# Second mixture: first pair by plain blocks, products ahead of sums, gates behind, operand steps in another order

## The chip, the cores and the metric

One core of one Trainium2 chip runs the kernel. Its engines are TensorE (PE in the rows, its weight loads PEld), VectorE (DVE), ScalarE (ACT), GpSimd (POOL) and SyncE (SP), which issues the transfers. Each engine works through its own queue in program order and waits there for what another engine has still to do. The metric is device microseconds of one execution; times are medians of several.

## The reference

Three stages follow each other. The change touches only the third.

```python
x = attention(q, k, v)                       # 4 x 576 tokens, 8 heads of 64 -> x: 2304 x 512
x = moe(x, phi, w1, w2)                      # first mixture: 8 experts of 4 slots each
# x is now  c @ slot_out : 2304 x 32 times 32 x 512
# second mixture:
logits = x @ w_gate                          # 2304 x 8
P = np.exp(logits - logits.max())
for _ in range(8):                           # the gates
    P /= P.sum(1, keepdims=True) + 1e-09
    P /= P.sum(0, keepdims=True) + 1e-09
    P *= N / E
out = 0
for e in range(8):
    h = np.maximum(x @ w1[e], 0.0)           # 2304 x 1024
    out += P[:, e:e + 1] * (h @ w2[e])       # 2304 x 512
```

All of it is in 4-byte floats.

## The kernel before

The second mixture (from line 777 on) never forms x. It takes x as c times the 32 slot outputs: `a_part` and `a_sum` (lines 802 to 823) form slot_out times w1[e] for one half of its 1024 columns each (`ap`, `as`), and `z_mm` (868) multiplies that by c to get the hidden layer of a pair. A **pair** is 256 tokens, two tiles of 128. An expert has nine pairs, eight experts have 72. A pair has 8 `z` matmuls, four for each half (z1 and z0, one buffer in PSUM for each).

The product with w2[e] is done by Strassen's scheme in Winograd's form: the pair's hidden layer is cut in 2 x 2 blocks a11, a12, a21, a22 and w2[e] in 2 x 2 blocks, and seven block products j0 to j6 (`product`, 918) stand in for eight. Every operand is split in a high and a low part (each rounded to the fast float form), so that a product is 12 matmuls: 84 for a pair. For the splitting, ACT makes the high part (`z_hi`, `s_hi`, and `w_hi` for the weights), DVE or POOL the low part (`z_lo` on DVE, `s_lo` on POOL, `w_lo` on either). Four operands are sums of blocks s1 to s4 (`z_sum` on DVE; h22 and h11 are copies of blocks on ACT, `z_f`, which two of the sums read). Of the weights, t1 to t4 are sums of blocks (`w_sum`); W0 to W6 are the operands of j0 to j6.

The results are added to `acc` on DVE by five updates for a pair: `up_a` behind j1, `up_b` behind j3, `up_d` behind j4, `up_c` behind j5, `up_e` behind j6 (940 to 954). j3 and j5 write to the bank that `up_a` and `up_b` read, j6 to the one that `up_d` reads. Four banks of PSUM (`qy`) serve the products, `ap`, `as` and the gates.

The order is written out by hand: every step of the mixture is entered into `plan` with a time in units of one product (12 matmuls), seven units for a pair, and the steps are issued in the order of these times (lines 1053 to 1118). With t0 the time of a pair's j0, line 1065 puts its z1 matmuls into t0-4 to t0-3, line 1066 its z0 matmuls into t0-3 to t0-2, and a table behind them has the operand steps. In the first expert the gates (`gate`, 976; `sink`, 1002) run as 130 side steps, one every five or six products, from the first pair on (`side_step`, 1070); their additions and divisions are on DVE. The weights of the next expert are loaded (`load_w1`, `load_w2`), multiplied (`a_part`, `a_sum`) and split (`w_plan`, 1089 to 1115) between the products of the expert before.

The first pair of all has nothing to run beside it: `a_part` and `a_sum` for both halves, t1 to t4, all the splits of its weights and its seven products follow each other directly behind the first mixture (1024 to 1043 and 1098 to 1102).

Of the kernel before, what the change touches and what calls it, by code (L numbers as in the profile page):

```python
# [46 lines left out]
WIDE_Q = frozenset((0, 2, 3, 9, 12, 13,))  # L47


@with_exitstack  # L50
def attn_moe_moe_kernel(
# [13 lines left out]
    nc = tc.nc  # L65
# [726 lines left out]
    def load_w1(e, i):  # L792
        t = wp.tile([128, KD, 512], FP32, name="w1s", tag="w")
        nc.sync.dma_start(out=t, in_=w1b[e, :, 512 * i:512 * i + 512].rearrange("(j p) f -> p j f", p=128))
        w1t[e, i] = t

    def load_w2(e, i):
        t = wp.tile([128, HF, DM], FP32, name="w2s", tag="w")
        nc.sync.dma_start(out=t, in_=w2b[e, 512 * i:512 * i + 512, :].rearrange("(j p) d -> p j d", p=128))
        w2t[e, i] = t  # L800

    def a_part(e, a):

        ap = qy.tile([128, 512], FP32, name="ap", tag="y")
        for j in range(KD):
            nc.tensor.matmul(
                out=ap[32 * j:32 * j + 32, :], lhsT=soT[:, j, 0, :], rhs=w1t[e, a][:, j, :], start=True, stop=True
            )
        s = op_.tile([128, 2, 512], FP32R, name="aps", tag="o")
        nc.scalar.activation(out=s[:, 0, :], in_=ap, func=ACTF.Copy)  # L810
        nc.vector.tensor_tensor(out=s[:, 1, :], in0=ap, in1=s[:, 0, :].bitcast(FP32), op=ALU.subtract)  # L811
        apt[e, a] = s

    def a_sum(e, a):
        ap = qy.tile([128, 512], FP32, name="as", tag="y")
        s = apt.pop((e, a))
# [7 lines left out]

    apt = {}
# [323 lines left out]
```

## Time and profile before

| what | value |
|---|---|
| median of 3 executions | 1137.19 us (1134.47 to 1137.31) |
| the profiled execution | 1138.38 us |
| its span, first to last instruction | 1136.5 us |
| mean granted TensorE clock | 0.961 |
| second mixture | from about 223 us to the end |
| PE, DVE, ACT, POOL busy over the span | 91%, 67%, 50%, 56% |

The page gives busy times of the whole span first, then 40 slices of it, the queues of the transfers, the chain of work that ended last, and the costliest groups of instructions. Busy shares over the span mix stages with different limits. The views by stretches of time (one row for each stretch) and the timelines of single engines show each stage by itself. In a timeline, the bracket at a row's end is the idle time of the engine before that row and what ended it.

### The profile page before, as it was taken

The numbers are of one execution on the slowest core, as the hardware profiler recorded it, in microseconds if no ns is written. First come the engines' busy times: TensorE is split into PE (matmuls) and PEld (weight loads), VectorE is DVE, ScalarE is ACT, GpSimd is POOL, SyncE is SP. The second block draws the span as 40 slices with busy tenths as digits, with TensorE's granted clock in tenths as the row PEclk, the third lists the DMA queues.
The fourth block names the chain that finished last, engine by engine and source line by source line (L and its number), as shares of the span: only waits on it lengthen the run. The fifth ranks groups of instructions, "written<-read, shape, count | busy, mean of one in ns | idle before, by whom it ended". The sixth has DMA issues, their size and how long they took to land.

```text
span 1136.5 us, 22853 instructions
## 1 busy us (share of the span) xinstructions
PE 1035.0 (91%) x9231; PEld 943.4 (83%) x9231; DVE 758.6 (67%) x1322; ACT 564.7 (50%) x1084; POOL 639.0 (56%) x488
## 2 busy tenths in 40 slices
PE   6888888859888999999989998999899989998998
PEld 5766653348778989998989998899889988998998
DVE  4997943176889766566667666666766676666665
ACT  5886731043335555654555455445544554455443
POOL 5654521065265637753965486558646763777353
PEclk9898978859999999999999999999899999999999
DMA  9999998930001300130013002201120120000111
GB/s 193 170 184 224 243 361 297 386 125 33 1 1 38 112 1 2 38 112 1 1 48 102 1 4 73 75 1 38 41 73 1 38 83 30 1 1 20 38 57 57
DMA packets 95901, 93.83 MB, mean 83 GB/s; under 512 B 59060, under 2 KB 64820, under 8 KB 95796
## 3 DMA queue, kind: packets, MB, share of 16 engines
q1 hardware_dynamic: 95796, 92.37, 29.5%
q8 instruction: 73, 1.20, 0.5%
q14 instruction: 32, 0.26, 0.1%
HBM read 87.64 MB, written 4.72 MB: 81 GB/s over the span
## 4 chain that ended last, share of the span: by engine, by line
PE 52%; DVE 20%; ACT 8%; issue 7%; DMA 7%; POOL 4%; SPq 2%; ACTq 0%; DVEq 0%; POOLq 0%
PE y L925 41%; DVE ft L898 6%; PE z L873 4%; DVE ot L888 4%; DVE acc L936 4%; DMA kn<-in_k_dram 3%; ACT wt L857 2%; ACT ft L894 2%; POOL wt L861 2%; PE h L711 1%; ACT ot L904 1%; DMA w2s<-in_moe_w_dram 1%; DVE bd L405 1%; DMA wa<-in_moe_w_dram 1%; POOL ot L908 1%
## 5 line engine op out<-in xcount | busy, mean ns | idle before, releaser
L925 PE MATMUL y<-wt,ot 128*128 128x256 f32 x6048 | 822.6, 286 | 50.6 <-DVE acc L936 36.3
L925 PEld LDWEIGHTS y<-wt,ot 128*128 128x128 f32 x6048 | 779.0, 193 | 74.8 <-issue 45.3
L908 POOL TENSOR_TENSOR ot<-ft,ot 128x512 fp32r<-128x512 f32 x288 | 372.9, 1315 | 343.9 <-ACT ot L904 337.6
L936 DVE SCALAR_TENSOR_TENSOR acc<-y,pg,acc 128x256 f32<-128x256 f32 x315 | 201.7, 640 | 150.1 <-PE y L925 149.9
L904 ACT ACTIVATE ot<-ft 128x512 fp32r<-128x512 f32 x288 | 166.8, 624 | 182.5 <-DVE ft L898 167.2
L898 DVE SCALAR_TENSOR_TENSOR ft<-z,ft 128x512 f32<-128x512 f32 x288 | 196.8, 683 | 12.2 <-ACT ot L884 11.7
L888 DVE SCALAR_TENSOR_TENSOR ot<-z,ot 128x512 fp32r<-128x512 f32 x216 | 148.0, 685 | 48.0 <-ACT ft L894 47.2
L884 ACT ACTIVATE ot<-z 128x512 fp32r<-128x512 f32 x216 | 128.1, 593 | 91.0 <-PE z L873 84.3
L873 PE MATMUL z<-c,a4s 128*128 128x256 f32 x576 | 163.1, 286 | 1.4 <-DVE a4s L823 1.4
L894 ACT ACTIVATE ft<-z 128x512 f32<-128x512 f32 x144 | 86.0, 597 | 148.8 <-DVE ot L888 79.2
L873 PEld LDWEIGHTS z<-c,a4s 128*128 128x128 f32 x576 | 110.8, 194 | 1.9 <-DVE a4s L823 1.9
L861 POOL TENSOR_TENSOR wt<-w2s,wt 128x1024 fp32r<-128x1024 f32 x23 | 56.8, 2482 | 10.8 <-ACT wt L857 10.8
L861 DVE TENSOR_TENSOR wt<-ts,wt 128x1024 fp32r<-128x1024 f32 x17 | 33.6, 1983 | 23.6 <-ACT wt L857 23.6
L861 POOL TENSOR_TENSOR wt<-ts,wt 128x1024 fp32r<-128x1024 f32 x15 | 42.3, 2839 | 5.9 <-ACT wt L857 5.9
L391 POOL TENSOR_TENSOR pl<-pl,l 128x384 f32<-128x384 f32 x16 | 13.3, 831 | 53.0 <-DVE l L387 51.5
L405 DVE STREAM_TRANSPOSE bd<-pl 32x384 f32<-32x384 f32 x64 | 36.4, 569 | 1.4
L847 POOL TENSOR_TENSOR ts<-w2s 128x1024 f32<-128x1024 f32 x15 | 37.0, 2464 | 0.0
L857 ACT ACTIVATE wt<-ts 128x1024 fp32r<-128x1024 f32 x32 | 32.8, 1046 | 6.0 <-DVE ts L847 6.0
L936 DVE SCALAR_TENSOR_TENSOR acc<-y,acc 128x512 f32<-128x512 f32 (+1 forms) x45 | 26.0, 577 | 11.7 <-PE y L925 11.5
L811 DVE TENSOR_TENSOR aps<-ap,aps 128x512 fp32r<-128x512 f32 x16 | 11.1, 692 | 28.3 <-ACT aps L810 28.3
L242 PE MATMUL kps<-ident,kn 96*128 96x96 f32 x96 | 13.2, 282 | 16.2 <-DMA kn<-in_k_dram 16.0
L257 ACT ACTIVATE kt<-kps 64x576 f32<-64x576 f32 x32 | 20.5, 642 | 13.9 <-DVE kd L249 13.7
(178 smaller groups left out, 826.8 us busy)
## 6 DMA issues: line engine op xcount, KB each, us to landing
wa<-in_moe_w_dram SPq DMA_DIRECT2D x32, 1024.0 KB, 9.8
w1s<-in_moe_w_dram SPq DMA_DIRECT2D x16, 1024.0 KB
w2s<-in_moe_w_dram SPq DMA_DIRECT2D x16, 1024.0 KB, 5.8
vw<-in_v_dram SPq DMA_DIRECT2D x62, 96.0 KB, 6.2
kn<-in_k_dram SPq DMA_DIRECT2D x32, 144.0 KB, 6.3
vg<-in_v_dram SPq DMA_DIRECT2D x16, 288.0 KB
out_dram<-acc SPq DMA_DIRECT2D x18, 256.0 KB, 2.0
qn<-in_q_dram SPq DMA_DIRECT2D x20, 144.0 KB, 6.6
```

Of the source, the lines that this page charges most:

```text
L405: nc.vector.transpose(out=bds[u % 2][32 * c:32 * c + 32, :, c, :], in_=U[u]["pl"][32 * c:32 * c + 32])
L857: nc.scalar.activation(out=t[:, 0], in_=w_of(e, i), func=ACTF.Copy)
L861: eng.tensor_tensor(out=t[:, 1], in0=w_of(e, i), in1=t[:, 0].bitcast(FP32), op=ALU.subtract)
L873: nc.tensor.matmul(out=zt[n, k][:, f, :], lhsT=a4s[:, e % 2, f0:f0 + 128], rhs=c4[:, BLK * b:BLK * b + BLK], start=True, stop=True,)
L884: nc.scalar.activation(out=t[:, 0], in_=zv(n, i, k), func=ACTF.Relu)
L888: nc.vector.scalar_tensor_tensor(out=t[:, 1], in0=zv(n, i, k), scalar=0.0, in1=t[:, 0].bitcast(FP32), op0=ALU.max, op1=ALU.subtract)
L894: nc.scalar.activation(out=t, in_=zv(n, i, k), func=ACTF.Relu)
L898: nc.vector.scalar_tensor_tensor(out=t, in0=zv(n, i, k), scalar=0.0, in1=ft[n, other], op0=ALU.max, op1=op)
L904: nc.scalar.activation(out=t[:, 0], in_=ft[n, name], func=ACTF.Copy)
L908: nc.gpsimd.tensor_tensor(out=t[:, 1], in0=ft[n, name], in1=t[:, 0].bitcast(FP32), op=ALU.subtract)
L925: nc.tensor.matmul(out=yt[n, bank][:, HD * half:HD * half + HD], lhsT=ot[n, name][:, l, f, :], rhs=tt[e, j][:, r, f, :], start=(m == 0 and ...
L936: nc.vector.scalar_tensor_tensor(out=o, in0=in_, scalar=pg[:, t, e:e + 1] if e else 1.0, in1=o, op0=ALU.mult, op1=ALU.add)
```

## The change

- The first pair is done by the plain scheme: eight products of blocks, 96 matmuls, with a fourth a-block (a21) and an eighth weight block (W7) in place of the four sums s1 to s4. It takes eight units where the other pairs take seven, so that all later times are one unit further on.
- `a_part` runs for both halves, the second half first, and `a_sum` follows for both. The gates' product `gp` and its split, which stood between them, become steps of the plan at 2.21 and 4.46, inside the first pair. `stack_r` and `ones` are made on POOL.
- The gates' side steps begin with the second pair, every five products, and are 118 in place of 130 (three tiles of the logits in one step). The logits, their transposed maxima and the maximum for all partitions share one bank.
- Within every pair all operand steps, the z1 matmuls and the updates have new times (`P`). z1 is issued 0.89 units earlier.
- The weights' steps have new times (`W0` for the first expert, `W` for the others). W1's low part goes from POOL to DVE. `a_part` begins about 0.9 units earlier in the expert than before, `a_sum` is 2.75 units later.
- The dictionaries of tiles become `Ring` objects, and `need` and `made` are assertions on the order; neither adds an instruction.

```diff
+P = {'z1': 4.89, 'z0': 3,
+ 'a12h': -2.46, 'a12l': -1.64, 'h22': -2.22, 'a11h': -2.12, 's1': -1.61, 'h11': -1.79, 'a11l': -1.49,
+ 'a22h': -1.24, 's2': -1.27, 'a22l': -0.3, 's2h': -0.05, 's2l': 0.24, 's4': 0.15, 's1h': -0.41, 's3': 0.65,
+ 's1l': 0.79, 's3h': 0.8, 's3l': 1.04, 's4h': 2.2, 's4l': 2.56,
+ 'ua': 2.01, 'ub': 4.22, 'ud': 5.2, 'uc': 6.19, 'ue': 7.47}
+P0 = ((-3.45, -3.16, -2.01, 1.77, -1.6, 2.91, -0.95, 0.59, 5.1, 6.1, 8.71, 8.08), ...
+W0 = {'0h': -9.21, '6h': -6.84, '1h': -4.85, '7h': -0.9, '2h': 2.44, '3h': 2.25, '4h': 3.75, '5h': 4.98,
+ 'gp': 2.21, 'g': 4.46,
+ '0l': (-8.05, 0), '6l': (-5.5, 1), '1l': (-2.28, 0), '7l': (1.08, 1),
+ 't1': (-7.68, 0), 't2': (-0.28, 1), 't4': (0.56, 1), 't3': (3.48, 0),
+ '2l': (2.5, 1), '3l': (5.33, 0), '4l': (4.74, 0), '5l': (5.44, 1)}
+W = {'ap': 14.61, 'as': 19.65,
+ 't1': (22.65, 1), 't2': (33.72, 1), 't4': (38.68, 1), 't3': (40.91, 1),
+ '0h': 44.89, '1h': 41.33, '2h': 57.7, '3h': 59.91, '4h': 56.58, '5h': 61.69, '6h': 66.19,
+ '0l': (48.68, 1), '1l': (45.62, 0), '2l': (59.61, 1), '3l': (62.44, 1), '4l': (59.48, 0), '5l': (65.8, 0),
+ '6l': (67.58, 1), 'ld1': 9.4, 'ld2': 9.71}
...
+    def plain(n, i, c, k, m):
+        if m == 0 and k == PLAIN_K[0]:
+            yt.tile((n, i, c), [128, DM], FP32, "y", "y")
+        f, p = divmod(m, 3)
+        l, r = ((0, 0), (1, 0), (0, 1))[p]
+        nc.tensor.matmul(
+            out=yt[n, i, c][:, 0:HD], lhsT=ot[n, f"a{i + 1}{k + 1}"][:, l, f, :],
+            rhs=tt[n // NB, PLAIN_T[k][c]][:, r, f, :],
+            start=(m == 0 and k == PLAIN_K[0]), stop=(m == 3 * HF - 1 and k == PLAIN_K[1]),
+        )
...
-    a_part(0, 0)
-    gp = qy.tile([128, E], FP32, name="gp", tag="y")
...
-    a_sum(0, 0)
-    a_part(0, 1)
...
-    a_sum(0, 1)
+    for i in (1, 0):
+        a_part(0, i)
+    for i in (1, 0):
+        a_sum(0, i)
...
-        t0 = 7 * n
+        t0 = 7 * n + min(n, nplain)
         for f in range(HF):
-            at(t0 - 4 + (f + 0.5) / 4, z_mm, n, 1, f)
-            at(t0 - 3 + (f + 0.5) / 4, z_mm, n, 0, f)
+            at(t0 - P["z1"] + (f + 0.5) / 4, z_mm, n, 1, f)
+            at(t0 - P["z0"] + (f + 0.5) / 4, z_mm, n, 0, f)
...
-                if e == 0 and (84 * n + 12 * j + m) % 11 in (5, 10):
-                    at(t0 + j + m / 12, side_step)
-        for t, f, *args in (
-            (-3.0, z_hi, "a12", 0, 1), (-2.9, z_lo, "a12", 0, 1), (-2.5, z_f, "h22", 1, 1),
-            (-2.0, z_hi, "a11", 0, 0), (-1.9, z_sum, "s1", 1, 0, "h22", ALU.add), (-1.6, z_f, "h11", 0, 0),
-            (-1.4, z_lo, "a11", 0, 0), (-1.2, z_hi, "a22", 1, 1), (-1.0, z_sum, "s2", 0, 0, "s1", ALU.subtract),
-            (-0.6, z_lo, "a22", 1, 1), (-0.5, s_hi, "s2"), (-0.4, s_lo, "s2"),
-            (-0.2, z_sum, "s4", 0, 1, "s2", ALU.add), (0.1, s_hi, "s1"), (0.3, z_sum, "s3", 1, 0, "h11", ALU.subtract),
-            (0.4, s_lo, "s1"), (0.8, s_hi, "s3"), (1.2, s_lo, "s3"), (1.4, s_hi, "s4"), (2.0, s_lo, "s4"),
-            (2.05, up_a), (4.05, up_b), (5.05, up_d), (6.05, up_c), (7.05, up_e),
+                if e == 0:
+                    step += 1
+                    if step % 10 in (4, 9):
+                        at(t0 + j + m / 12, side_step)
...
-        t0 = 7 * NB * (e - 1)
+        t0 = 7 * NB * (e - 1) + T1 - 7
...
-            e, ((t0 + 31.5, "t1", G), (t0 + 33.1, "t2", G), (t0 + 38.5, "t4", G), (t0 + 40.1, "t3", G)),
-            tuple(t0 + x for x in (44.5, 45.8, 57.2, 58.4, 59.5, 60.6, 61.7)),
-            tuple((t0 + x, g) for x, g in (
-                (45.5, G), (47.1, G), (59.5, G), (61.1, G), (60.0, V), (65.5, V), (66.5, G),
-            )),
```

In `W0` and `W` the second number of a pair names the engine: 0 is DVE, 1 is POOL.

## Rows read from the trace of the kernel before

**Rows 1.** Page, part 1: busy us, share of the span, instructions.
```profile
PE 1035.0 (91%) x9231; PEld 943.4 (83%) x9231; DVE 758.6 (67%) x1322; ACT 564.7 (50%) x1084; POOL 639.0 (56%) x488
```
**Rows 2.** Busy time by stretch: length, engines (instructions), granted clock, DMA share, GB/s.
```profile
core 0: us, PE busy (x) PEld busy (x) DVE busy (x) ACT busy (x) POOL busy (x), PEclk, DMA share, GB/s
230.00:240.00 10.00, 3.24 (x11) 2.31 (x10) 8.62 (x6) 3.11 (x5) 7.59 (x3) 0.50 0.00 0
250.00:260.00 10.00, 9.08 (x74) 8.71 (x74) 5.26 (x8) 3.96 (x7) 10.00 (x8) 1.00 0.82 307
272.30:377.40 105.10, 87.23 (x682) 81.64 (x681) 86.03 (x157) 42.38 (x71) 55.73 (x36) 0.98 0.04 11
498.12:607.19 109.07, 104.47 (x849) 100.83 (x849) 71.69 (x114) 54.31 (x93) 68.75 (x45) 1.00 0.12 40
1044.26:1133.10 88.84, 88.82 (x738) 88.61 (x738) 57.34 (x95) 38.94 (x69) 40.75 (x32) 1.00 0.13 49
```
**Rows 3.** The chain that ended last: start us, us, engine, tile, line, instructions.
```profile
498.12 6.01 PE y L925 x48
...
607.19 6.01 PE y L925 x48
...
1064.80 7.56 PE y L925 x63
1075.84 7.56 PE y L925 x63
```
**Rows 4.** Timeline of PE, first expert: start us, us, instruction [idle before <- releaser].
```profile
240.72 1.43 PE L925 MATMUL y<-wt,ot 128*128 128x256 f32 x5 [6.07 <-DVE ot L888]
...
246.41 1.22 PE L925 MATMUL y<-wt,ot 128*128 128x256 f32 x4 [2.33 <-DVE ot L888]
...
256.74 0.28 PE L873 MATMUL z<-c,a4s 128*128 128x256 f32 x1
...
269.22 0.28 PE L873 MATMUL z<-c,a4s 128*128 128x256 f32 x1
...
374.39 0.28 PE L873 MATMUL z<-c,a4s 128*128 128x256 f32 x1
```
**Rows 5.** Timeline of DVE at the start of the second mixture.
```profile
231.42 0.69 DVE L823 TENSOR_TENSOR a4s<-as,a4s 64x512 fp32r<-64x512 f32 x1 [1.24 <-ACT a4s L822]
232.14 1.23 DVE L847 TENSOR_TENSOR ts<-w2s 128x1024 f32<-128x1024 f32 x1
233.40 3.27 DVE L847 TENSOR_TENSOR ts<-ts,w2s 128x1024 f32<-128x1024 f32 x1
```
**Rows 6.** Groups of instructions on POOL, 223 to 262 us.
```profile
L861 POOL TENSOR_TENSOR wt<-w2s,wt 128x1024 fp32r<-128x1024 f32 x2 | 6.5, 3262 | 10.8 <-ACT wt L857 10.8
L1087 POOL MEMSET acc<- 128x2048 f32 (+1 forms) x4 | 6.3, 1590 | 0.0
L861 POOL TENSOR_TENSOR wt<-ts,wt 128x1024 fp32r<-128x1024 f32 x1 | 2.4, 2399 | 5.9 <-ACT wt L857 5.9
```
**Rows 7.** Waits from 380 us on: us in total, times, longest us.
```profile
ACT ft L894 <- DVE ot L888: 70.1, 62, 3.7
...
DVE ot L888 <- ACT ft L894: 41.1, 62, 0.7
...
PE y L925 <- DVE acc L936: 24.5, 18, 2.9
```
**Rows 8.** Timeline of DVE, second expert.
```profile
451.79 0.68 DVE L898 SCALAR_TENSOR_TENSOR ft<-z,ft 128x512 f32<-128x512 f32 x1
...
480.60 2.25 DVE L861 TENSOR_TENSOR wt<-ts,wt 128x1024 fp32r<-128x1024 f32 x1 [4.35 <-ACT wt L857]
482.77 0.74 DVE L936 SCALAR_TENSOR_TENSOR acc<-y,pg,acc 128x512 f32<-128x512 f32 x1
...
492.07 1.22 DVE L861 TENSOR_TENSOR wt<-ts,wt 128x1024 fp32r<-128x1024 f32 x1
```
**Rows 9.** Timeline of PE, second and third expert.
```profile
454.55 0.28 PE L873 MATMUL z<-c,a4s 128*128 128x256 f32 x1
...
483.66 6.42 PE L925 MATMUL y<-wt,ot 128*128 128x256 f32 x49 [2.94 <-DVE acc L936]
...
512.82 1.07 PE L806 MATMUL ap<-w1s,soT 128*32 128x512 f32 x8
...
521.81 0.63 PE L818 MATMUL as<-aps,stack_r 128*128 128x512 f32 x2
```

More of the change, by code (lines that the diff above doesn't have):

```diff
@@ L47, with __init__, tile, __contains__ @@
 WIDE_Q = frozenset((0, 2, 3, 9, 12, 13,))
+P = {'z1': 4.89,
+ 'z0': 3,
+ 'a12h': -2.46,
+ 'a12l': -1.64,
+ 'h22': -2.22,
+ 'a11h': -2.12,
+ 's1': -1.61,
+ 'h11': -1.79,
+ 'a11l': -1.49,
+ 'a22h': -1.24,
+ 's2': -1.27,
+ 'a22l': -0.3,
+ 's2h': -0.05,
+ 's2l': 0.24,
+ 's4': 0.15,
+ 's1h': -0.41,
+ 's3': 0.65,
+ 's1l': 0.79,
+ 's3h': 0.8,
+ 's3l': 1.04,
+ 's4h': 2.2,
+ 's4l': 2.56,
+ 'ua': 2.01,
+ 'ub': 4.22,
+ 'ud': 5.2,
+ 'uc': 6.19,
+ 'ue': 7.47}
+NPLAIN = 1
+P0 = ((-3.45, -3.16, -2.01, 1.77, -1.6, 2.91, -0.95, 0.59, 5.1, 6.1, 8.71, 8.08),
+ (-1.58, 2.82, -3.83, -10.07, -3.18, 3.82, 1.07, -4.42, 1.7, 2.01, 10.07, 9.98))
+W0 = {'0h': -9.21,
+ '6h': -6.84,
+ '1h': -4.85,
+ '7h': -0.9,
+ '2h': 2.44,
+ '3h': 2.25,
+ '4h': 3.75,
+ '5h': 4.98,
+ 'gp': 2.21,
+ 'g': 4.46,
+ '0l': (-8.05, 0),
+ '6l': (-5.5, 1),
+ '1l': (-2.28, 0),
+ '7l': (1.08, 1),
+ 't1': (-7.68, 0),
+ 't2': (-0.28, 1),
+ 't4': (0.56, 1),
+ 't3': (3.48, 0),
+ '2l': (2.5, 1),
+ '3l': (5.33, 0),
+ '4l': (4.74, 0),
+ '5l': (5.44, 1)}
+W = {'ap': 14.61,
+ 'as': 19.65,
+ 't1': (22.65, 1),
+ 't2': (33.72, 1),
+ 't4': (38.68, 1),
+ 't3': (40.91, 1),
+ '0h': 44.89,
+ '1h': 41.33,
+ '2h': 57.7,
+ '3h': 59.91,
+ '4h': 56.58,
+ '5h': 61.69,
+ '6h': 66.19,
+ '0l': (48.68, 1),
+ '1l': (45.62, 0),
+ '2l': (59.61, 1),
+ '3l': (62.44, 1),
+ '4l': (59.48, 0),
+ '5l': (65.8, 0),
+ '6l': (67.58, 1),
+ 'ld1': 9.4,
+ 'ld2': 9.71}
+class Ring:
+    def __init__(self, pool, bufs):
+        self.pool, self.bufs, self.count, self.kept = pool, bufs, {}, {}
+    def tile(self, key, shape, dtype, name, tag):
+        t = self.pool.tile(shape, dtype, name=name, tag=tag)
+        self.count[tag] = self.count.get(tag, 0) + 1
+        self.kept[key] = t, tag, self.count[tag]
+        return t
+    def __contains__(self, key):
+        return key in self.kept
+    def __getitem__(self, key):
+        t, tag, i = self.kept[key]
+        return t
 @with_exitstack
@@ L921, in product @@
         if m == 0 and j in (0, 2):
-            yt[n, bank] = qy.tile([128, DM], FP32, name="y", tag="y")
+            yt.tile((n, bank), [128, DM], FP32, "y", "y")
+        need(("o", n, name), ("wl", e, j))
+        made.add(("y", n, j, m))
         f, p = divmod(m, 3)
@@ L1117, in attn_moe_moe_kernel @@
+            at(t0 + W["as"] + 2 * i, a_sum, e, i)
+        for name in ("t1", "t2", "t4", "t3"):
+            t, g = W[name]
+            at(t0 + t, w_sum, e, name, (V, G)[g])
+        for i in range(7):
+            at(t0 + W[f"{i}h"], w_hi, e, i)
+            t, g = W[f"{i}l"]
+            at(t0 + t, w_lo, e, i, (V, G)[g])
     for _, _, f, args in sorted(plan, key=lambda x: x[:2]):
```

243 lines of the change are left out of this document (156 added, 87 removed).

## The prediction

> **What bounds the kernel now.** The page's busy times name PE: 1035.0 of 1136.5 us, against 758.6 on DVE [rows 1]. That is an average over stages, so the second view is the busy time by stretch [rows 2], which shows three regimes in the second mixture. In the last stretch, 1044.26 to 1133.10, PE is busy for 88.82 of 88.84 us: no wait at all. The chain that ended last gives the period there, 1075.84 - 1064.80 = 11.04 us for a pair [rows 3]; with 84 + 8 matmuls that is 0.120 us each, and it is the floor of a pair, which no order of the operands lowers. In the stretch 498.12 to 607.19, which is one full cycle of an expert (nine pairs, one round of `ap` and `as`, one round of weight splits; the chain returns to the same work at both ends [rows 3]), PE is idle for 4.6 us. In the first expert, 272.3 to 377.4, it is idle for 17.9 of 105.1 us, and DVE is busy for 86.03, or 82%. So there are three stretches to cost: start, rest of the first expert, six full cycles. The last expert's tail has nothing to give.
>
> Pair boundaries in the first expert come from the last z matmul of a pair: it stands 25.5 products before j0, 3.06 us. The second pair begins near 260.0, the third at 272.3, the tenth at 377.45 [rows 4].
>
> **A: the start, up to the third pair.** At present `as` of the second half ends its split at 232.1 and the DVE queue then holds three weight sums (1.23, 3.27, about 3.2) ahead of a12's low part [rows 5]; the first pair's products wait 6.07 us for it, and 2.33 us more for a later one [rows 4]. The first pair takes 26 us. In the new order the second `a_part` follows the first directly instead of behind an `a_sum`, which I estimate brings the last z of the pair some 2 to 3 us forward, to about 230.3. Ahead of a12's low part DVE has only W0's low part and t1. One such step takes 1.2 alone and 3.3 beside POOL [rows 5, 6]; with W0l at 229.4 to 230.7 and t1 to 233.5, a12l ends near 234.2. Plain products then run on it, two of them to about 237; a22l stands behind W1l (to 237) and a21l, so it ends at 238.2. The next block waits for it. `gp` needs so4 behind a22l, and its bank is wanted by the fourth plain bank, so that PE also waits there for `gp`'s split, which is queued on DVE behind t3: near 242. This is a wait that the change adds; behind it in PE's queue are half of the plain products. From there six plain products at 1.44 and the next pair's eight z (0.96) give 242 + 8.6 + 1.0 = 251.6 for the second pair's j0, unless W7's low part on POOL (W6l, t2, t4 at 3.3, one memset 1.6, W7l 2.4 to 3.3: near 245) [rows 6] is later than the sixth product, which it is not. I take 250.5.
>
> The second pair has the four sums again. POOL works in order: W7l 245, two memsets and W2l to 250, two memsets and W5l to 255, then s2l, at 1.3 each after that to 259.5. So j3 starts near 255.5, j6 at 259.7, and the third pair at about 262. Everything alone (1.2 on DVE, 2.4 on POOL) gives 257, everything contended 267. Sum of A: 272.3 to 262, that is -10 (-15 to -5). The 12 extra matmuls (1.44 us) and a21's splits are in it, and so are the four memsets, which cost POOL 6.3 us [rows 6] ahead of operands that PE waits for. The loads of the next expert go about three units later on SP; nobody is queued behind them, and `ap` comes five units after.
>
> **B: pairs three to nine.** DVE does the same 86.0 us of work [rows 2] plus W1l (1.2 to 2.25), some 88 us, against a PE floor of 7 x 11.04 + 3.4 = 80.7 (`ap` 2 x 1.07 and `as` 2 x 0.63 [rows 9]). An in-order DVE queue never packs fully: 19.1 us of the 105.1 are idle now. A part of that is the ping-pong on the z tiles: ACT's copies of blocks wait for DVE's low part of another block (70.1 us from 380 us on, 62 times) and DVE's low part for ACT (41.1) [rows 7], because the steps on one z tile alternate between engines. The new order puts the four ACT steps a12h, h22, a11h, h11 ahead and lets DVE do a12l, s1, a11l, s2 in one run, so those waits should go, and the ninth pair is left free of gates. Against that the gates are denser: the same eight rounds in 7 pairs instead of 8.5. I take half of the idle time as recovered, 88 + 10 = 98, -7. Bounds: 104 (only the ninth pair gains, denser gates cost it back) to 91 (one idle microsecond in three).
>
> **C: six full cycles.** Floor of one: 9 x 11.04 + 3.4 = 102.8; it takes 109.07 [rows 2], so 6.3 us are waits and what follows them. The largest is at the weight round: W4's low part on DVE waits 4.35 us for ACT, takes 2.25 beside POOL, and `up_b` behind it in the queue comes at 482.77, so that PE stands for 2.94 us [rows 8, 9]. All of PE's waits for updates are 24.5 us in the six cycles [rows 7]. In the new order W4h is issued about three units earlier and W4l directly behind `up_a`. Counted from a pair's j0 on PE: `up_a` ends at 3.7, `up_b` can begin at 6.4 (j3 has ended), j5 wants its bank at 8.2. W4l fits there alone (1.22 [rows 8]) and beside POOL (2.25) with `up_b` at 6.4 either way. W1l and W5l are put in the same gap. At W6's low part the margin is thin: POOL has s2l to s4l to 7.1 and W6l to 9.5, and j6 wants it at 9.8. `up_a` in the pair behind `as` ends with nothing to spare. So I leave 1.8 of the 6.3 and take 4.5 a cycle, 6 x -4.5 = -27 (all 6.3: -38; only the 2.94 less a new wait of 0.5: -15).
>
> The trace has the price of one more two-input step on DVE beside POOL: 2.25 instead of 1.22 [rows 8]. The Trainium skill ("SBUF — State Buffer", section "SBUF: two separate sides") says that such a step and a GpSimd step hold the shared port exclusively, the loser waiting for the whole instruction. That speaks against moving W1l to DVE: if POOL's row of four low parts kept the port until 7.1, W1l and W4l would end at 8.3, `up_b` at 9.0 and j5 would lose 0.8 twice a cycle, 10 us in all, 1104 instead of 1094; the 2.25 us row shows a wait of one POOL step only, so the sum stays.
>
> **The sum.** 1138.4 (the profiled execution's own time; its span is 1136.5, with 1.9 around it) - 10 - 7 - 27 = 1094.4. That execution lies 1.2 above the median of 1137.19, so on the median's scale 1093.
>
> **Rivals.**
> 1. Same mechanisms, smaller yield: A -5, B 0 because denser gates leave DVE as full as before, C -15: 1117. For it: DVE is 82% busy in B already. With values between, 1107 to 1118. Chance 0.20.
> 2. Slower by the single z1 buffer. s4 is the last reader of z1. It now ends at 452.5, and the next pair's z1 begins at 454.55: 2.1 us of room [rows 8, 9]. The new order issues z1 0.89 units earlier, 1.3 us, and leaves s4's place in the DVE queue, so 0.8 us remain. If DVE runs later than that, PE waits with the z1 matmul at the head of its queue, in every pair. It decides from 0.8 us of lateness; at 1.6 us it costs 0.8 x 63 = 50 us from pair ten on, hides the cycle gains in part (-10 left of them) and keeps A: 1138 - 10 - 10 + 50 = 1168. For it: first expert, where DVE is full. Against: with the ping-pong gone DVE should run earlier, not later. Chance 0.08; with pairs of both kinds anything above 1141, 0.03 more.
> 3. The gain is hidden: W6l, `up_a` and `gp`'s split become the new waits and take it all, 1134 to 1140. Chance 0.04.
> 4. The clock. PE's granted clock is 0.50 in 230 to 240 and 1.00 in 250 to 260, that is 1.2 and 2.4 GHz [rows 2]; it rose behind the first dense products. If it stays low through the whole plain pair, 104 matmuls at 0.24 take 25 us from 234, the third pair is at 271 and A is -1: 1102. The Trainium skill ("TensorE: Matmul & The Clock Gate", "What's actually happening") says that activity releases the throttle; earlier dense work would then raise it earlier, and A stays at -10. Chance 0.07, inside the range.
>
> **How the numbers follow.** The forecast, 1079 to 1107, has 0.53; rival 1 has 0.20, rival 4 0.07, more than the forecast (C at its floor, B at 91) 0.05, rival 3 0.04, slower cases 0.11. The range takes in the forecast, rival 4 and rival 1: 1076 to 1118. Faster by over 0.3% (3.4 us, about what a measurement of this kernel can tell from no change): 0.53 + 0.20 + 0.07 + 0.05 = 0.85; within 0.3%: 0.04; slower: 0.11.
>
> **What would show it.** A: z of the second pair begins before 246 and the third pair's j0 stands near 262; wrong if PE's wait for `gp`'s split is over 3 us. B: waits of ACT's block copies for DVE nearly gone, the tenth pair near 360. C: a cycle of 103.5 to 106 us, PE's waits for updates below 1 us in it. The last eight pairs stay at 11.04 us each; a longer period there means rival 2, and would break the forecast alone.

## The result and the profile after

| | before | after |
|---|---|---|
| median of 4 executions each, taken together | 1135.83 us (1133.32 to 1137.31) | 1093.59 us (1089.72 to 1093.97) |
| ratio of the times | 1 | 0.962, 95% interval 0.959 to 0.965 |
| profiled execution | 1138.38 us | 1093.25 us |
| its span | 1136.5 us | 1091.5 us |

The forecast was 1093. The total is right and its three terms are not. The page's busy times of the changed kernel, against [rows 1], and its chain, in shares of the span by engine; the last line is the chain of the kernel before:

```profile
PE 1024.3 (94%) x9243; PEld 943.9 (86%) x9243; DVE 757.4 (69%) x1322; ACT 566.8 (52%) x1080; POOL 625.6 (57%) x481
...
PE 78%; DVE 11%; DMA 5%; ACT 2%; POOL 2%; issue 1%; SPq 1%; POOLq 0%; ACTq 0%; DVEq 0%
...
PE 52%; DVE 20%; ACT 8%; issue 7%; DMA 7%; POOL 4%; SPq 2%; ACTq 0%; DVEq 0%; POOLq 0%
```

DVE is busy for about as long as before (757.4 and 758.6 us), but has 11% of the chain instead of 20%. Where that happens is seen in the busy time by stretch (columns as in [rows 2]): first one cycle of an expert, then pairs three to nine, then two slices of the plain pair.

```profile
498.12:600.78 102.66, 102.66 (x851) 100.54 (x850) 71.11 (x116) 54.84 (x93) 67.17 (x44) 1.00 0.13 42
269.05:372.90 103.85, 89.87 (x686) 85.25 (x686) 89.63 (x164) 43.24 (x74) 51.43 (x35) 0.95 0.03 11
...
235.00:240.00 5.00, 5.00 (x24) 5.00 (x25) 5.00 (x4) 3.37 (x6) 4.92 (x3) 0.50 0.00 0
...
245.00:250.00 5.00, 4.56 (x21) 4.56 (x22) 1.58 (x4) 1.80 (x3) 5.00 (x3) 0.50 0.71 235
```

The cycle has no PE wait at all: 102.66 of 102.66 us, where it was 104.47 of 109.07 [rows 2]. Pairs three to nine of the first expert take 103.85 us, nearly what they took. PE idles 14.0 us there where it idled 17.9 [rows 2], but its granted clock is 0.95 against 0.98, and it is busy for 89.87 us against 87.23. DVE is busy for 86% of the stretch.

To compare runs I read one mark for each pair, the last of its z matmuls (as [rows 4]; it stands 25.5 matmuls, 3.06 us, ahead of j0, and not 25.5 products of 12 matmuls), and count from the copy to soT that ends the first mixture. That copy starts anywhere from 214.0 to 225.5 us in the profiled executions below, whatever was changed behind it; so two or three microseconds between medians can be the stretch ahead of the change, and the columns from soT on tell more. Between the two profiles of before and after, 2.5 us of the difference stand ahead of that copy (223.1 and 220.6).

| kernel | median | soT to 2nd pair | 2nd to 3rd | 3rd to 10th | steady cycle |
|---|---|---|---|---|---|
| before | 1135.8 | 33.6 | 12.5 | 105.2 | 109.07 |
| after | 1093.6 | 32.3 | 13.1 | 103.9 | 102.66 |
| x1, pair order of before | 1103.4 | 31.9 | 13.1 | 110.2 | 103.4 |
| x2, weights' times of before | 1132.3 | 33.1 | 13.1 | 103.8 | 106.6 to 109.2 |
| x3, two gate rounds | 1073.5 | 33.1 | 13.1 | 88.2 | 102.66 |
| x4, 30 more matmuls at the start | 1089.0 | 30.5 | 13.1 | 103.1 | 102.66 |
| x5, gates at fixed places | 1085.5 | 31.1 | 13.6 | 101.2 | 102.65 |
| x6, gp ahead | 1085.9 | 27.2 | 13.1 | 103.1 | 102.66 |
| x7, W4's steps of before | 1094.9 | 31.1 | 13.1 | 103.1 | 103.28 |
| x8, before with the new weights' times | 1100.0 | 32.3 | 12.5 | 109.8 | 103.4 |
| x9, z1 one unit earlier | 1132.7 | 28.5 | 13.1 | 109.0 | 108.37 |
| x10, splits' times of before | 1121.4 | 31.1 | 13.1 | 103.8 | 105.64 |
| x11, gp ahead and gates spread | 1074.1 | 24.2 | 13.6 | 90.9 | 102.66 |
| x12, W4's steps and W3h of before | 1116.8 | 30.9 | 13.1 | 103.1 | 105.64 |

Two of x2's ten executions, the profiled one among them, are in a slower state (1137.2 and 1137.8 us), and its ratio below leaves them out.

In the two profiles of before and after, A is therefore -0.7 where -10 was forecast (33.6 + 12.5 against 32.3 + 13.1), B is -1.3 where it was -7, and everything from the tenth pair on is 745.3 - 704.9 = -40.4 where C was -27. The 704.9 us of after are the floor worked out ahead: 62 x 11.04 + 6 x 3.4 = 704.9.

### The profile page after: what moved, and what is told of

It reads as the page before. It is cut to its first block, busy times and chain, and to the rows that moved or that the text cites. A ratio compares the mean times of both kernels' runs of the same rounds, so it can differ in the third digit from the quotient of the medians.

```text
span 1091.5 us, 22939 instructions
## 1 busy us (share of the span) xinstructions
PE 1024.3 (94%) x9243; PEld 943.9 (86%) x9243; DVE 757.4 (69%) x1322; ACT 566.8 (52%) x1080; POOL 625.6 (57%) x481
## 4 chain that ended last, share of the span: by engine, by line
PE 78%; DVE 11%; DMA 5%; ACT 2%; POOL 2%; issue 1%; SPq 1%; POOLq 0%; ACTq 0%; DVEq 0%
PE y L1038 62%; PE z L980 6%; PE ap L909 2%; PE h L810 2%; DVE bd L504 1%; DVE ft L1007 1%; DMA w1s<-in_moe_w_dram 1%; DVE ot L996 1%; DMA wa<-in_moe_w_dram 1%; DMA vw<-in_v_dram 1%; DVE acc L1072 1%; PE loc L563 1%; DMA kn<-in_k_dram 1%; PE y L1051 1%; DVE pg L1173 1%
## 5 line engine op out<-in xcount | busy, mean ns | idle before, releaser
L1038 PE MATMUL y<-wt,ot 128*128 128x256 f32 x5964 | 798.0, 284 | 11.8 <-DVE acc L1072 8.9
L1038 PEld LDWEIGHTS y<-wt,ot 128*128 128x128 f32 x5964 | 763.4, 193 | 26.5 <-issue 19.8
L1017 POOL TENSOR_TENSOR ot<-ft,ot 128x512 fp32r<-128x512 f32 x284 | 378.7, 1354 | 319.9 <-ACT ot L1013 187.9
L1013 ACT ACTIVATE ot<-ft 128x512 fp32r<-128x512 f32 x284 | 172.3, 628 | 177.9 <-DVE ft L1007 169.9
L1007 DVE SCALAR_TENSOR_TENSOR ft<-z,ft 128x512 f32<-128x512 f32 x284 | 193.4, 681 | 0.2
L970 POOL TENSOR_TENSOR wt<-w2s,wt 128x1024 fp32r<-128x1024 f32 x16 | 38.7, 2419 | 9.2 <-ACT wt L963 9.2
L970 POOL TENSOR_TENSOR wt<-ts,wt 128x1024 fp32r<-128x1024 f32 x16 | 39.1, 2463 | 0.0
L963 ACT ACTIVATE wt<-ts 128x1024 fp32r<-128x1024 f32 x32 | 33.6, 1053 | 7.6 <-DVE ts L950 3.3
L1072 DVE SCALAR_TENSOR_TENSOR acc<-y,acc 128x512 f32<-128x512 f32 (+1 forms) x44 | 24.6, 562 | 18.2 <-PE y L1038 13.4
L950 POOL TENSOR_TENSOR ts<-w2s 128x1024 f32<-128x1024 f32 x14 | 33.7, 2408 | 0.0
L499 ACT ACTIVATE pd<-pd,ls 72x144 f32<-72x144 f32 x64 | 21.3, 407 | 9.4 <-DVE ls L485 8.2
L963 ACT ACTIVATE wt<-w2s 128x1024 fp32r<-128x1024 f32 x25 | 26.0, 1047 | 0.0
```

Of the source, the lines that this page charges most:

```text
L963: nc.scalar.activation(out=tt[e, i][:, 0], in_=w_of(e, i), func=ACTF.Copy)
L1007: nc.vector.scalar_tensor_tensor(out=t, in0=zv(n, i, k), scalar=0.0, in1=ft[n, other], op0=ALU.max, op1=op)
L1013: nc.scalar.activation(out=t[:, 0], in_=ft[n, name], func=ACTF.Copy)
L1017: nc.gpsimd.tensor_tensor(out=t[:, 1], in0=ft[n, name], in1=t[:, 0].bitcast(FP32), op=ALU.subtract)
L1038: nc.tensor.matmul(out=yt[n, bank][:, HD * half:HD * half + HD], lhsT=ot[n, name][:, l, f, :], rhs=tt[e, j][:, r, f, :], start=(m == 0 and ...
L1072: nc.vector.scalar_tensor_tensor(out=o, in0=in_, scalar=pg[:, t, e:e + 1] if e else 1.0, in1=o, op0=ALU.mult, op1=ALU.add)
```

## The experiments

**Which part carries it: order within the pairs or the weights' times.** x1 puts the table `P` back, x2 the table `W`; x8 puts the new `W` alone into the kernel before.

```diff
x1: -P = {'z1': 4.89, 'z0': 3, 'a12h': -2.46, ...   +P = (times of before; z1 of the first pair stays)
x2: -W = {'ap': 14.61, 'as': 19.65, ...             +W = (times and engines of before)
x8: the kernel before, with the times and engines of the new W
```

> The changed kernel with the operand steps and updates of every pair (z1 of the first pair aside) back at the times of the kernel before; the weights' steps keep their new times. Theory 1 (the cycles' gain comes from where the weights' steps stand, because undisturbed pairs took 11.04 us in the kernel before too): a full cycle stays at 102.7 to 103.7 us and the time at 1094 to 1102 us. Rival (the order within the pair carries it, through the waits of ACT and DVE for each other on the z tiles): a cycle near 106 to 109 us and 1112 to 1130 us, and ACT's block copies wait for DVE again for some 100 us in all.

> The changed kernel with all weights' steps of the later experts (loads, ap, as, sums, splits) back at the times of the kernel before, W1's low part on POOL again; the pairs keep their new times. Theory 1 (weights' steps carry the cycles' gain): a cycle of 106 to 109 us, with PE waiting 2 to 3 us for an update behind W4's low part, 1114 to 1132 us. Rival (order within the pair carries it): a cycle below 104 us, 1094 to 1102 us.

> The kernel before with only the weights' steps of the later experts at their new times and W1's low part on DVE; first pair, gates and pairs as before. Theory (the start and the gates' places bring nothing, the weights' steps bring the cycles): a cycle of 103.4 to 104 us as with the old pair times in the changed kernel, and the same time as there, 1100 to 1106 us. Rival (the plain first pair brings the 10 us that I forecast for it): 1110 to 1116 us.

Measured: x1 0.973 of before (interval 0.969 to 0.977), x2 0.996 (0.992 to 1.0005), x8 0.969 (0.965 to 0.973). The cycles came as theory 1 had them in all three; the times of x1 and x2 lie at the upper edge of its ranges or just over, that of x8 at the lower edge. The weights' times carry most: they bring the cycle from 109.07 to 103.4 by themselves. On top of them the order within the pairs brings the last 0.75 us of a cycle and 6.3 us in the first expert (110.2 to 103.9). With the start and the gates of the kernel before, x8 is as fast as x1, so the plain start and the new places of the gates bring about nothing.

x2's executions lie from 1118.6 to 1137.8 us, and its cycles from 106.6 to 109.2. Both go with the granted clock: the two executions at a mean of 0.965 and 0.966 took 1120.0 and 1118.6 us, the others, at 0.949 to 0.956, 1129.5 or more. In the profile PE waits 2.79 us for an update in the third cycle and again in the fifth. The timeline of PE and the clock (columns as in [rows 2]) behind each wait:

```profile
594.52 6.35 PE L1020 MATMUL y<-wt,ot 128*128 128x256 f32 x51 [2.79 <-DVE acc L1054]
594.50:600.50 6.00, 5.98 (x50) 6.00 (x51) 5.77 (x10) 2.20 (x5) 3.69 (x3) 1.00 0.52 175
...
809.16 8.97 PE L1020 MATMUL y<-wt,ot 128*128 128x256 f32 x51 [2.79 <-DVE acc L1054]
809.10:815.20 6.10, 6.04 (x28) 6.07 (x29) 5.45 (x10) 2.04 (x4) 3.76 (x3) 0.50 0.50 170
```

The same wait left the clock at full speed once, and at half of it the other time, which cost 2.62 us more. With the clock at 1.00 throughout, x2's cycle is 106.57, still 2.5 us shorter than before's. So the pairs' order gains 2.5 us a cycle beside the old weights' times and 0.75 beside the new ones: the two parts take up some of the same waits.

x1 also judges the ping-pong on the z tiles. The waits of x1 from 380 us on (total, times, longest), then those of after:

```profile
ACT ft L980 <- DVE ft L984: 52.9, 62, 1.2
ACT ft L980 <- DVE ot L973: 51.8, 62, 0.8
```
```profile
ACT ot L992 <- DVE ot L996: 21.3, 50, 0.5
```

In x1 more than 100 us of ACT waits are back, and a cycle is 0.75 us longer, so they cost that at most. Here the waits of an engine that is not the bottleneck cost next to nothing, however large their sum.

**Which of the weights' steps.** x7 puts back W4's two steps alone, x10 all fourteen splits, and x12 is x7 with one more step put back: W3's high part.

```diff
x7:  '4h': 56.58 -> 59.5    '4l': (59.48, 0) -> (60.0, 0)
x10: '0h' to '6h' and '0l' to '6l': times and engines of before
x12: as x7, and '3h': 59.91 -> 58.4
```

> The changed kernel with only W4's two parts back at the times of the kernel before (high part 59.5, low part 60.0 in the expert). Theory (the largest wait of a cycle is this one step, queued on DVE ahead of up_b while its high part is not made): PE waits 2 to 3 us for an update once in each cycle, which goes from 102.7 to 105 to 106 us, 1109 to 1118 us. Rival (the waits came from several steps together, and one of them alone is taken up by slack): below 1098 us.

> The changed kernel with only the seven weight splits (0h to 6h, 0l to 6l) of experts 2 to 8 at their places of before, W1l on POOL again; ap, as, the four weight sums and the loads stay at their new places. Theory (the splits carry the gain of the cycles, the sums and ap and as little): cycles of 106 to 108 us against 102.66, time 1115 to 1130. Rival (the gain comes from the sums, ap and as being moved; all weights' steps at their old places gave 1132): cycles of 103 to 104, time 1094 to 1104.

> The changed kernel with W4's two steps at their places of before (as in the run with W4 alone, 1094.9) and, as the one further edit, W3's high part at its place of before too, so that it stands ahead of W4's high part on ACT. Theory (the order of the two ACT steps decides: W4l then starts one microsecond later, falls beside W2's low part on POOL and takes 2.9 instead of 1.5 us, and up_b stands behind it): PE waits 2.6 to 2.9 us for an update once a cycle instead of 0.45, cycles of 105.4 to 106 against 103.3, time 1111 to 1118. Rival (the wait with all splits at their old places needs W2l and W3l on POOL to be early too): PE waits below 1 us, cycles of 103.3, time 1093 to 1097.

x7 is 0.962 of before (0.960 to 0.964), as its rival said: hardly a loss against after (0.6 us a cycle), which spoke against W4l as the carrier. x10 is 0.989 (0.985 to 0.992), with one wait a cycle; its time is in the theory's range. x12, 0.986 (0.980 to 0.992) and as its theory said, shows why both are true. The timelines of the weight round, x7 first: ACT (two instructions, W4h then W3h), DVE (W4l), POOL (W2l and W3l), PE.

```profile
570.99 2.00 ACT L963 ACTIVATE wt<-ts 128x1024 fp32r<-128x1024 f32 x2
...
572.07 1.47 DVE L970 TENSOR_TENSOR wt<-ts,wt 128x1024 fp32r<-128x1024 f32 x1 [2.79 <-ACT wt L963]
...
572.42 5.75 POOL L970 TENSOR_TENSOR wt<-ts,wt 128x1024 fp32r<-128x1024 f32 x2
...
574.35 6.34 PE L1038 MATMUL y<-wt,ot 128*128 128x256 f32 x51 [0.45 <-DVE acc L1072]
```

The same work in x12, where the two ACT steps are W3h, then W4h:

```profile
576.34 1.99 ACT L963 ACTIVATE wt<-ts 128x1024 fp32r<-128x1024 f32 x2
...
578.37 2.88 DVE L970 TENSOR_TENSOR wt<-ts,wt 128x1024 fp32r<-128x1024 f32 x1 [3.73 <-ACT wt L963]
...
577.77 5.71 POOL L970 TENSOR_TENSOR wt<-ts,wt 128x1024 fp32r<-128x1024 f32 x2
...
582.05 6.34 PE L1038 MATMUL y<-wt,ot 128*128 128x256 f32 x51 [2.80 <-DVE acc L1072]
```

Read from the start of the ACT pair: W4l starts at 1.08 us in x7 and is ahead of POOL's W2l by 0.35 us; it takes 1.47. In x12 it starts at 2.03, 0.60 behind POOL's start, and takes 2.88. So one ACT step of 0.95 us ahead of W4h costs 0.95 + 1.41 = 2.36 us, and PE's wait grows by 2.80 - 0.45 = 2.35 us: the whole of it reaches PE through `up_b`, which stands behind W4l on DVE. x12 and x10 have the same cycle, 105.64, so of all the splits that stand at their old places in x10 none adds anything to this order in the steady cycles. In the changed kernel W4h is further ahead still, and W4l waits for nothing:

```profile
569.49 1.06 ACT L963 ACTIVATE wt<-ts 128x1024 fp32r<-128x1024 f32 x1 [0.45 <-PE y L1038]
...
571.47 1.35 DVE L970 TENSOR_TENSOR wt<-ts,wt 128x1024 fp32r<-128x1024 f32 x1
```

By the medians, x2 loses 11 us beyond x10. The six cycles of the two profiles are as far apart, and about half of that is the granted clock. The other half, 0.9 us a cycle (106.57 against 105.64 with the clock at 1.00 in both), belongs to `ap`, `as`, the sums and the loads: a second wait of PE for an update, 0.69 us, stands there in x2. I did not take these steps apart further.

**The single z1 buffer (rival 2).** x9 moves z1 one unit further ahead.

```diff
-            at(t0 - P["z1"] + (f + 0.5) / 4, z_mm, n, 1, f)
+            at(t0 - (5.9 if n else 4.89) + (f + 0.5) / 4, z_mm, n, 1, f)
```

> The changed kernel with one number moved: the z1 products of every pair after the first are issued 5.9 instead of 4.89 units ahead of the pair, about 1.5 us earlier on PE. Theory (the single z1 buffer is a real limit that the new order passes with room of about one microsecond): s4, the last reader of z1, now ends after the z1 products want the bank, PE waits 0.4 to 0.7 us in each of 62 pairs, the period goes from 11.04 to about 11.5 us and the time from 1093.6 to 1118 to 1136. Rival (DVE has slack and simply runs earlier): period 11.04, 1090 to 1097.

x9: 1132.7 us, 0.998 of before (0.996 to 1.0001), in the theory's range: the whole gain is gone. PE's waits over the second mixture, then s4 on DVE and the z1 matmul behind it:

```profile
PE z L980 <- DVE ft L1007: 38.0, 61, 3.1
...
487.70 0.68 DVE L1007 SCALAR_TENSOR_TENSOR ft<-z,ft 128x512 f32<-128x512 f32 x1
...
488.53 0.36 PE L980 MATMUL z<-c,a4s 128*128 128x256 f32 x1 [0.57 <-DVE ft L1007]
```

The same two instructions in the changed kernel:

```profile
569.49 0.68 DVE L1007 SCALAR_TENSOR_TENSOR ft<-z,ft 128x512 f32<-128x512 f32 x1
...
571.09 0.28 PE L980 MATMUL z<-c,a4s 128*128 128x256 f32 x1
```

s4 ends at 570.17 and z1 begins at 571.09: 0.92 us of room. From the tenth pair on the room is never under 0.85 us. The change runs that close to a limit that costs 39 us when it is passed by 0.6 us a pair. In the first expert it is passed: four times z1 begins 0.06 us behind the end of s4, and in two of them PE waited noticeably, 2.3 us in all. PE's waits for it from 230 to 380 us (total, times, longest):

```profile
PE z L980 <- DVE ft L1007: 2.3, 2, 1.6
```

**The start: clock or waits.** x4 adds 30 matmuls that nothing reads, 10 ahead of the first `ap` and 20 between the first z matmuls and the plain pair's products; x6 takes `gp` and its split out of the plain pair and puts them ahead of `ap` and between `ap` and `as`.

```diff
x4: +    warm("warm1", 10)        # ahead of a_part
    +    at(-0.6, warm, "warm2", 20)
x6: +    gate_part()
         for i in (1, 0): a_part(0, i)
    +    g_copy()
         for i in (1, 0): a_sum(0, i)
    -    at(W0["gp"], gate_part)
    -    at(W0["g"], g_copy)
```

> The changed kernel with 30 more matmuls on PE that write a bank nobody reads: 10 in the wait for the first weights' transfer, 20 between the first z matmuls and the first product. Theory (the plain pair is slow because PE's clock is granted at 0.67 in 230 to 250 us, half of its matmuls at 0.21 us): the clock is 1.00 from about 236 us, the second pair begins 2 to 4 us earlier, 1089 to 1092 us. Rival (the plain pair waits for its operands and the clock is hidden behind them): within 1 us of 1093.6, or up to 2 us later for the added matmuls.

> The changed kernel with the gates' product put back ahead of the first a_part, where PE waits for the first weights and DVE idles, and its split behind both. Theory (in the first pair its DVE copy takes 3.15 us beside POOL instead of 0.42 and PE waits 1.2 us for it and 1.3 us for the split): the second pair begins 2.5 to 5 us earlier counted from the slots' outputs, 1089 to 1091 us. Rival (POOL's weight splits bound the first two pairs): within 1 us of 1093.6.

The waits in the changed kernel's plain pair, on PE's timeline:

```profile
222.81 3.09 PE L909 MATMUL ap<-w1s,soT 128*32 128x512 f32 x16 [2.24 <-DMA w1s<-in_moe_w_dram]
...
231.83 0.39 PE L1051 MATMUL y<-wt,ot 128*128 128x256 f32 x1 [1.85 <-ACT ot L992]
234.72 5.92 PE L1051 MATMUL y<-wt,ot 128*128 128x256 f32 x26 [2.51 <-DVE ot L996]
241.85 1.06 PE L1194 MATMUL gp<-wg_sb,so 128*128 128x8 f32 x8 [1.21 <-DVE so L1191]
245.44 1.01 PE L1051 MATMUL y<-wt,ot 128*128 128x256 f32 x3 [1.34 <-DVE g L1203]
```

With x4 the stretch from soT to the second pair is 30.5 us. Kernels that don't touch the plain start have 28.5 to 33.1 there, so the extra matmuls show nothing. x4 is 0.960 of before (0.957 to 0.964), where after is 0.962 (0.959 to 0.965); that 1089.0 us lies in the theory's range is luck, since the clock did not stay at 1.00. It is higher from 230 to 240 us, but falls back behind the wait for a12l (2.28 us there), and the wait for so4 grows to 2.35 us. The stretch in after, then in x4:

```profile
230.00:240.00 10.00, 5.66 (x25) 5.46 (x26) 9.97 (x7) 5.44 (x9) 8.29 (x4) 0.68 0.00 0
```
```profile
230.00:240.00 10.00, 5.57 (x33) 5.31 (x33) 9.97 (x8) 5.46 (x7) 8.71 (x5) 0.83 0.01 2
```

x6 has 27.2 us from soT to the second pair, 1.3 below the lowest of those kernels, and is 0.955 of before (0.951 to 0.959), 1085.9 us where its theory had 1089 to 1091. x11, with the same start, has 24.2, so the stretch as a whole varies. What x6 shows is clear in the part behind the wait for a12l: from there to the second pair's last z it needs 11.9 us and x11 11.4, after 18.2 and the other kernels with `gp` in the plain pair 15.7 to 18.6. The waits for so4 and for the split inside the pair are gone. That part of PE's timeline in x6 (its last z is at 252.69; in after it goes from 234.72 to 252.90), and DVE's copy so4 in before, after and x6:

```profile
240.83 7.35 PE L1051 MATMUL y<-wt,ot 128*128 128x256 f32 x38 [2.52 <-DVE ot L996]
```
```profile
223.72 0.42 DVE L1030 COPY so<-soT 128x512 f32<-128x512 f32 x1
```
```profile
238.64 3.15 DVE L1191 COPY so<-soT 128x512 f32<-128x512 f32 x1
```
```profile
225.85 0.56 DVE L1187 COPY so<-soT 128x512 f32<-128x512 f32 x1
```

**The gates in the first expert.** x3 leaves six of the eight rounds out; x5 keeps all, each at fixed places of a pair instead of every five matmuls (the description of the change says products); x11 joins x6 with a better spread (two rounds in the fourth and fifth pair, none in the ninth) and folds the factor N/E into the eight column factors, one DVE step less a round.

```diff
x3:  -        for _ in range(8):      +        for _ in range(2):
x5:  -  if step % 10 in (4, 9): at(t0 + j + m / 12, side_step)
     +  one round a pair, from 13.3 + 7 i, its column part at 17.05 + 7 i; the eighth from 59.06
x11: x6, and rounds from 13.3, 20.3, 27.3, 31.1, 34.6, 41.3, 48.3, 55.3
     -  tensor_scalar(cs_, cs_, EPS, add)     +  tensor_scalar(cs_, cs_, EPS, E / N, add, mult)
     -  tensor_scalar(pg, pg, N / E, mult)
```

> The changed kernel with two rounds of the gates' normalisation instead of eight; six rounds are left out. Theory (the gates' work on DVE is what holds up pairs three to nine of the first expert): those seven pairs fall from 103.9 to about 84 to 90 us, 1074 to 1080 us in all, and PE's waits for updates in the first expert (8.9 us) nearly go. Rival (the first expert is held up by the start, the clock or the weights): 1090 us or more.

> The changed kernel with the gates' side steps at other times, one round for a pair: the column part behind up_a of a pair, where DVE idles until up_b, the row part of the next round behind up_d, the sum's matmul just ahead of the next pair. Nothing is left out. Theory (pairs three to nine are slow because the gates' operations stand in DVE's queue ahead of updates that PE waits for, not because DVE has too much to do): those seven pairs fall from 103.9 to about 88 to 95 us, 1078 to 1086 us in all. Rival (DVE has too much to do there, 86% busy, and any order of it gives the same): 100 to 105 us for the seven pairs, 1090 to 1096 us in all.

> The two repairs together: gp and its split ahead of a_part and a_sum of the first expert, and the eight gate rounds at fixed places of pairs (two of them in the fourth to fifth pair, none in the ninth); the scaling of the gates by N/E is folded into the eight column factors, which takes one DVE step from each round. Theory (both costs are separate: 5.4 us from the end of the first mixture to the second pair, and 5 to 9 us in pairs three to nine): 1074 to 1081. Rival (the two share the same wait, or the dense rounds cost again what they save): 1083 to 1088.

x3 is 0.948 of before (0.944 to 0.952) and x11 0.947 (0.944 to 0.950), both near what their theories said. x5 is 0.955 (0.952 to 0.958); its time fits its theory, but its seven pairs take 101.2 us, as its rival said, and 6.4 us of its profile's gain over after stand ahead of the copy to soT. The stretch of pairs three to nine, in x3 and in x11 (columns as above):

```profile
268.23:356.45 88.22, 84.53 (x673) 81.82 (x671) 63.48 (x110) 43.33 (x73) 49.58 (x34) 0.96 0.04 13
```
```profile
259.28:350.14 90.86, 84.69 (x683) 80.85 (x681) 80.48 (x154) 43.08 (x74) 49.32 (x33) 1.00 0.04 13
```

Without the six rounds DVE has 26 us less to do and the stretch is 15.6 us shorter. x11 has all eight rounds and is within 2.6 us of it, at 89% DVE. DVE's busy time is 9 us less there (6.7 of it is the folded step, eight times 0.23 to 1.21 us), and the stretch is 13.0 us shorter. PE idles 6.2 us in it instead of 14.0, and at a granted clock of 1.00 instead of 0.95 its own work takes 5.2 us less. In the changed kernel the gates' steps stand ahead of an update that PE wants. DVE and PE there:

```profile
289.54 2.17 DVE L1173 TENSOR_TENSOR pg<-pg,cs 128x144 f32<-128x144 f32 x1
291.75 1.18 DVE L1174 TENSOR_SCALAR pg<-pg 128x144 f32<-128x144 f32 x1
292.84 0.41 DVE L1072 SCALAR_TENSOR_TENSOR acc<-y,acc 128x256 f32<-128x256 f32 x1
...
293.40 3.33 PE L1038 MATMUL y<-wt,ot 128*128 128x256 f32 x14 [3.70 <-DVE acc L1072]
296.53 0.41 PE L980 MATMUL z<-c,a4s 128*128 128x256 f32 x1
```

x5's eighth round, pressed in beside the weight round, made PE stand for 6.2 us. Of the 13.0 us that x11 gains here over after, x5, which moves the rounds and takes no work away, has 2.7; the better spread and the shorter round bring the rest, and these two were not taken apart. So it is argued and not shown that the place of the rounds gives most of it. The waits of x5's PE:

```profile
PE sp L1163 <- DVE pg L1159: 7.4, 2, 6.2
```

x11, 1074.1 us, is 19.5 us faster than the changed kernel and the fastest with the whole computation.

## Why the prediction was right in sum and wrong in its terms

That the sum came out right is luck. Against the forecast, A fell 9.3 us short and B 5.7, and C gave 13.4 more; another 2.5 us of the profiles' difference stand ahead of the change.

**A, the start: the step that failed is the estimate of DVE in the plain pair.** The waits were named rightly (a12l, `gp`, its split: 2.51, 1.21 and 1.34 us). But so4, a copy that I gave no term of its own, takes 3.15 us beside POOL, and DVE has no gap from 230.6 to 246.6, so `gp`'s split comes late. Counted from the copy to soT, forecast and measured are 7.2 and 9.1 us for the first pair's last z, 18.9 and 24.8 for the end of `gp`'s split, 24.3 and 32.3 for the second pair's last z, 38.9 and 48.4 for the third pair's j0. So the new order of `a_part` brought the first pair forward by 1.6 us (10.7 to 9.1), less than the 2 to 3 that I estimated. That its last z stands at 229.7, where I had 230.3, and that the second pair's z matmuls begin at 246.3, near the mark of 246, is luck: that copy came 2.5 us earlier. From `gp`'s split to the second pair's last z PE works mostly at half the clock. The wait that was to prove A wrong, `gp`'s split above 3 us, did not come; A was lost to several small waits and to the clock. x6 and x11 show that `gp` inside the pair cost 4 to 7 us.

**Rival 4, the clock, holds in part.** PE's granted clock is 0.50 in 235 to 240 and in 245 to 250 us, that is 1.2 GHz, and 0.74 from the copy to soT to the second pair's last z (before: 0.64); it falls behind waits. The price was a little high: a matmul at the half clock takes 0.22 us (14 from 293.40 to 296.53, above), not 0.24.

```profile
220.61:252.90 32.29, 22.41 (x115) 17.95 (x115) 21.61 (x19) 13.33 (x18) 21.80 (x11) 0.74 0.35 126
```
```profile
223.13:256.74 33.61, 21.69 (x112) 16.37 (x113) 23.76 (x27) 14.86 (x22) 18.43 (x8) 0.64 0.48 166
```

The Trainium skill ("TensorE: Matmul & The Clock Gate", section "What's actually happening") says that activity releases the throttle, which I had taken to mean that earlier dense work keeps A whole. The trace of x4 agrees that it raises the clock (0.83 against 0.68 from 230 to 240 us), but A is not kept by it: the clock fell again behind the next wait.

**B, pairs three to nine: one term left out, the clock behind the waits.** PE idles 3.9 us less in this stretch, but its own work takes 2.6 us longer at the lower clock; the tenth pair's j0 comes at 372.9, not near 360. The recovery I gave to the new pair order, -7, is there: x1 against after is -6.3. What I missed is that the kernel with the new weights' times is slower here: x8, with before's order and gates, needs 109.8 us where before needs 105.2, 4.7 more. That is not more waiting. The stretch in x8:

```profile
258.70:368.55 109.85, 93.30 (x683) 89.22 (x681) 89.50 (x162) 43.12 (x73) 53.73 (x35) 0.91 0.03 11
```

PE idles 16.6 us there, 1.3 less than in before, but is busy for 93.3 us with the same work, at a clock of 0.91 against 0.98 [rows 2]. W1l on DVE was in my sum with its 1.2 to 2.25 us; whether it moves the waits so that the clock falls, or whether other executions would show less, one profile of each kernel cannot tell. By their lengths, x8 and x1 (109.8 and 110.2) show no cost of the denser gates, which I feared; by its idle time x1 has 2.1 us more. Yet the gates can give much of the 13 us of x11: the idle time that I saw in this stretch belonged for the most part to a piece that the change only shifts.

The reason given for B was not shown either. The ACT waits on the z tiles did go, as forecast, but in the steady cycles they were not what PE waited for: 0.75 us a cycle at most, by x1.

**C, the cycles: the wait was named rightly, the size was too small.** W4l in the gap before `up_b`, with its high part made in time: this is what x12 shows to be worth 3.0 us a cycle (105.64 against 102.66), about half of the 6.4 that a steady cycle gains. It is not the three units by which W4h moves: x7 puts W4's steps back and loses 0.6 us. What counts is that W4h stands ahead of W3h on ACT, and W3h moved too. The mis-sized term is what I left: 1.8 of 6.3 us for thin margins at W6l and at `up_a` behind `as`. They hold: the only wait of PE from 380 us on is 0.3 us in all.

```profile
PE y L1038 <- POOL wt L970: 0.3, 1, 0.3
```

By the marks, the six cycles take 616.6 us instead of 652.1, -35.5: the first of them had only 105.9 to begin with, the other five give 6.4 to 7.2 each. The other 4.9 us come from the stretch behind the sixth cycle, 88.4 instead of 93.3. I had said that the tail has nothing to give, from a stretch that begins at 1044 [rows 2]; the wait of the last weight round lies just ahead of that.

**The lock on the shared port.** The Trainium skill ("SBUF — State Buffer", section "SBUF: two separate sides") says that the loser waits for the whole instruction of the other engine. The 1104 us came from my own addition, that a row of POOL steps keeps the port. In x12, W4l begins 0.60 us inside POOL's W2l, which ends at 580.16; W4l ends 1.1 us later, at 581.25, and POOL's next step takes 3.37 us instead of 2.4. In x7, W4l begins first and takes 1.47, and there POOL's W2l takes 3.37. POOL's two steps in x12, then W2l in x7:

```profile
577.77 2.39 POOL L970 TENSOR_TENSOR wt<-ts,wt 128x1024 fp32r<-128x1024 f32 x1
...
580.11 3.37 POOL L970 TENSOR_TENSOR wt<-ts,wt 128x1024 fp32r<-128x1024 f32 x1
```
```profile
572.42 3.37 POOL L970 TENSOR_TENSOR wt<-ts,wt 128x1024 fp32r<-128x1024 f32 x1
```

So the traces agree with the rule: the loser waits for the rest of one instruction and is let in between two of them. Here that makes it decisive to start ahead of POOL; in the changed kernel W4l does, and takes 1.35 us.

**The other rivals.** Rival 1 came nearer than the forecast on A and B and was wrong on C. Rival 2 did not happen from the tenth pair on, but x9 shows that the limit is real: 0.92 us of room where I had read 0.8, and beyond it 38 us of waits in 61 pairs. In the first expert, where I had said that DVE is full, it did happen, for 2.3 us. Rival 3 would have needed new waits in the cycle; there are none.

## What to carry to other kernels

When an in-order engine serves a bottleneck, ask of each step what stands behind it in its queue and what stands ahead of it on the engine that it waits for: here one copy of 1 us on ACT decides 2.4 us of PE in every cycle, while 100 us of waits off the path decide at most 0.75. A sum that comes out right can still hide terms that are wrong in both directions; only putting parts back one at a time told them apart. Side work on a nearly full engine is better placed by the gaps of its queue than at even distances, and first of all made shorter; how much each gives was not separated here. Before a time is put down to work or waits, look at the granted clock of the stretch: in this kernel it moves single stretches by several microseconds with the same work.

## What the runs showed of the hardware

A DVE copy of 128 x 512 from SBUF to SBUF takes 0.42 us with POOL idle (before), 0.56 where it begins beside the end of a memset (x6) and 3.15 us beside POOL's weight sum and a memset (after). A product of 128 x 144 in the gates of after takes 0.31 us with POOL idle (at 314.3) or 2.17 beside it (at 289.5). Such small steps are as exposed to POOL as the large ones, and I had priced only the large ones. After PE's wait of 3.70 us at 289.7, the next 14 matmuls took 3.13 us, 0.22 each, the half clock, where the same work takes 0.120 each in the steady cycle. So a wait can be paid for twice, but need not be: of two waits of 2.79 us in x2, one was followed by half the clock and the other was not.
